# Second and third unit of a fast convolution: PSUM copies ahead of SiLU calls on ScalarE, and three matmuls of the next unit in front of product 6

## The chip, the cores and the metric

The kernel runs on one core of one Trainium2 chip. The metric is device time in microseconds (us) for one execution. A core has five engines with a queue each: TensorE (PE in the profile; its weight loads are listed apart as PEld), VectorE (DVE), ScalarE (ACT), GpSimd (POOL) and SyncE (SP), which here only issues DMAs. An engine runs its instructions in the order in which they stand in the program; between engines, semaphores say when an instruction may start.

## The reference

A convolution over the sequence with three taps, a batch normalisation with given mean and variance, and SiLU:

```python
B, S, C = 2, 2048, 1024; K = 3
xp = jnp.pad(x, ((0, 0), (1, 1), (0, 0)))
y = sum(jnp.einsum('bsc,cd->bsd', xp[:, k:k + S, :], w[k]) for k in range(K))
y = (y - mean) * (g / jnp.sqrt(var + 1e-5)) + b
return silu(y)
```

x is 2 x 2048 x 1024, w is 3 x 1024 x 1024, all in bfloat16.

## The kernel before

**The method.** Six output rows at a time are made from eight input rows by a Winograd scheme F(6,3). One sequence gives 342 such tiles of six rows. The input is transformed into eight planes (T_sb, one per batch entry); the three taps of the weights are turned into eight planes too, of which planes 0 and 7 are raw taps (wch) and planes 1 to 6 are sums and differences that GpSimd makes (uch). For each plane a product over the 1024 input channels follows, and the eight products are combined into six output rows.

**Units.** A unit is 128 output channels (dc, 0 to 7) of one batch entry (bi, 0 or 1). Units run in the order (0,0), (0,1), (1,0), (1,1), ...; here they are counted from 0, so "the second and third unit" are units 1 and 2. Units 0 to 14 are made by `unit`; the last one has code of its own (`last_part`). Each of a unit's eight products is eight accumulating matmuls of 128 x 342 (`mms`, L255), which `mms` yields one by one, so that `run(gen, n)` can emit n matmuls of a unit between other work.

**One unit.** It has four PSUM banks, A, B_, C_ and G; even and odd units use different halves of the eight. The products come in the order 1, 3, 2, 4, 5, 7, 6, 0. Product 1 goes to A and ScalarE copies it out (m1), then product 2 is added onto it in A, so product 2 must wait for copy m1. In the same way product 4 follows copy m3 (bank B_) and product 6 follows copy m5 (bank C_). Copies s1 and s2 save A after product 2 and B_ after product 4. VectorE combines all this into the six rows y (L296), in a tile `y` that has one buffer for all units, and at last ScalarE applies SiLU with the normalisation's scale and shift (L266) into yT.

**The queue of ScalarE.** The three SiLU calls of a unit (rows 2 and 4; rows 1, 3 and 5; row 0) are not issued at the unit's end but put on the list `late`. The next unit takes them from there: ahead of each of its five copies, in the order m1, m3, s1, s2, m5, `copy_out` takes as many entries of `late` as the tuple `pace` says, and after m5 the rest is taken (`while late`). `late` also holds, behind the SiLU calls, the issue of the unit's output (a transposing DMA and stores, L425 to L443, all on SyncE's queue) and, in unit 1, the scaled tap w0x (L151, ScalarE) with GpSimd's last sums for the next weights.

**Unit 0 and the transforms.** Unit 0 is emitted in pieces between the transforms. While the second batch entry is transformed (17 windows, three transforms each, 51 in all, counted by gi), `want` says how many matmuls of unit 0 are out after each transform. Unit 0 also splits products 7 and 0 by columns: a first part comes early, and eight narrow matmuls of 128 x 111 of product 7 stand just before product 6. Behind the transforms, L409 to L411 issue weight loads on SyncE, and L412 emits the rest of unit 0. Units 1 to 14 follow in a loop (L454 to L484); ahead of a unit with bi = 0 stands VectorE's sum of two taps (L169), ahead of one with bi = 1 the scaling of taps on ScalarE (L151) and GpSimd's sums.

Of the kernel before, what the change touches and what calls it, by code (L numbers as in the profile page):

```python
# [37 lines left out]
def kernel(  # L38
# [14 lines left out]
    CT = C // P  # L53
# [30 lines left out]
    def load_weights(dp):  # L84
        open_weights(dp)
        for k in (0, 2, 1):
            nc.sync.dma_start(out=pair_tile[dp][:, k], in_=w_all[:, k, :, dp * 2 * P:(dp + 1) * 2 * P])
# [160 lines left out]
    def mms(bk, j, dc, bi, c0, c1, start, at=0):  # L248

        for ct in range(CT):  # L250
            if j in (0, 7):
                lhsT = raw[dc][0 if j == 0 else 2][:, ct, :]
            else:
                lhsT = wts[dc][:, j - 1, ct, :]
            nc.tensor.matmul(  # L255
                ps_all[:, bk * 512 + at:bk * 512 + at + c1 - c0],
                lhsT=lhsT,
                rhs=T_sb[bi][:, ct, j, c0:c1],
                start=start and ct == 0,
                stop=ct == CT - 1,  # L260
                skip_group_check=not start,
            )
            yield
# [7 lines left out]
            scale=sk[:, dc:dc + 1],  # L271
        )

    def unit(dc, bi, c0, c1, banks, yT, late, pace=(1, 0, 1, 1, 0), cut=None, calls=None):

        nn = c1 - c0
        A, B_, C_, G = [ps_all[:, k * 512:k * 512 + nn] for k in banks]
        bA, bB, bC, bG = banks
        pace = list(pace)

        def et(name):
            return epool.tile([P, NTB], FP32, name=name)[:, 0:nn]

        m1, m3, m5, s1, s2, d1 = (et(n) for n in ("m1", "m3", "m5", "s1", "s2", "d1"))
        y_all = epool.tile([P, M_OUT, NTB], FP32, name="y")[:, :, 0:nn]
        y = [y_all[:, i if calls is None else ENDS.index(i)] for i in range(M_OUT)]

        def stt(o, i0, s, i1, op1=ALU.add):
            nc.vector.scalar_tensor_tensor(out=o, in0=i0, scalar=s, in1=i1, op0=ALU.mult, op1=op1)  # L296
            load["dve"] += 0.00123 * nn

        def copy_out(dst, src):
            for _ in range(pace.pop(0)):  # L300
                if late:
                    late.pop(0)()
            nc.scalar.copy(dst, src)  # L303
            load["act"] += 0.001 * nn

        if cut:


            p0 = et("s2")
            yield from mms(bG, 7, dc, bi, c0, c0 + cut, True)  # L310
            yield from mms(bC, 0, dc, bi, c0, c0 + cut, True)
            yield from mms(bC, 0, dc, bi, c0 + cut, c1, True, cut)
            copy_out(p0, C_)
        yield from mms(bA, 1, dc, bi, c0, c1, True)
        copy_out(m1, A)
        yield from mms(bB, 3, dc, bi, c0, c1, True)
        copy_out(m3, B_)
        yield from mms(bA, 2, dc, bi, c0, c1, False)
        copy_out(s1, A)
        stt(d1, m1, 2.0, A, op1=ALU.subtract)  # L320
        yield from mms(bB, 4, dc, bi, c0, c1, False)
        if cut:
            stt(y[0], B_, ALPHA, p0)
            stt(y[2], B_, ALPHA * 4.0, s1)
            nc.vector.tensor_tensor(y[0], A, y[0], op=ALU.add)
            stt(y[4], B_, ALPHA * 16.0, s1)
        else:
            copy_out(s2, B_)
            for i in (2, 4):
                stt(y[i], B_, ALPHA * 2.0 ** i, s1)  # L330
        stt(B_, m3, 2.0, B_, op1=ALU.subtract)
        yield from mms(bC, 5, dc, bi, c0, c1, True)
        copy_out(m5, C_)
        while late:
            late.pop(0)()
        for i in (1, 3, 5):
            stt(y[i], B_, ALPHA * 2.0 ** i, d1)
        if cut:
            yield from mms(bG, 7, dc, bi, c0 + cut, c1, True, cut)
        else:  # L340
            yield from mms(bG, 7, dc, bi, c0, c1, True)
        nc.vector.tensor_tensor(y[5], G, y[5], op=ALU.add)  # L342
        yield from mms(bC, 6, dc, bi, c0, c1, False)
        for i in (2, 4):
            stt(y[i], C_, BETA * 0.5 ** i, y[i])
        stt(G, m5, 2.0, C_, op1=ALU.subtract)
        if not cut:
            yield from mms(bA, 0, dc, bi, c0, c1, False)
        for i in (1, 3, 5):
            stt(y[i], G, BETA * 0.5 ** i, y[i])  # L350
        if cut:
            stt(y[0], C_, BETA, y[0])
        else:
            stt(y[0], s2, ALPHA, A)
            stt(y[0], C_, BETA, y[0])

        if calls is None:
            late.extend(lambda i=i: silu(dc, yT, y_all, c0, c1, *i, 2) for i in ((2, 5), (1, 6), (0, 1)))
        else:
            late.extend(lambda i=i: silu(dc, yT, y_all, c0, c1, *i) for i in calls)  # L360
# [10 lines left out]
    with tc.tile_pool(name="xwin", bufs=10) as xpool:  # L371
        first = unit(0, 0, 0, NTB, (0, 1, 2, 3), yTs[0], late, cut=11 * WT)
        for wi in range(NWIN):
            window = load_window(xpool, 0, wi)
            if wi in (3, 8, NWIN - 1):
                load_chunk(0, {3: 2, 8: 0, NWIN - 1: 1}[wi])
            for h in range(2):
                bk = (2 * wi + h) % 4 * 2 if wi < 10 else (0, 6, 4)[(2 * wi + h - 20) % 3]
                transform(0, wi, window, 4 * h, 4, bk, 2, 2 if h == 0 and wi in (4, 9) else 0)
            if wi == 0:  # L380
                turn_params()
            if wi == 5:
                open_chunk(0)
                scale_weights(0, (2,), on_gpsimd=True)
            if wi == 8:
                pair_sum(0, 0)
                pair_sum(0, 1)
                scale_weights(0, (0,), on_gpsimd=True)
                pair_sum(0, 2)

            run(first, {13: 2, 14: 2, 15: 4, 16: 8}.get(wi, 0))
        pair_tap(0, 0, ALU.add)
        scale_weights(0, (1,), on_gpsimd=True)
        for n, op in ((1, ALU.add), (0, ALU.subtract), (1, ALU.subtract), (2, ALU.add), (2, ALU.subtract)):
            pair_tap(0, n, op)
        make_params()
        load["act"] = load["dve"] = 0.0
        gi, done = 0, 0


        for wi in range(NWIN):
            window = load_window(xpool, 1, wi)
            for ct0, n in ((0, 3), (3, 3), (6, 2)):
                transform(1, wi, window, ct0, n, 4 + gi if gi < 4 else (4, 5, 6, 7, 2)[(gi - 4) % 5], 3)
                gi += 1
                want = 8 * gi // 3 if gi < 4 else 8 + 20 * (gi - 3) // (3 * NWIN - 3)
                run(first, want - done)
                done = want
        for k in (0, 2, 1):  # L409
            load_chunk(1, k)  # L410
        load_weights(1)  # L411
        run(first)  # L412

    opool = ctx.enter_context(tc.tile_pool(name="opool", bufs=3))
# [32 lines left out]
    def finish(dc, bi, yT):  # L447

        turned.append(turn(dc, bi, yT))
        if len(turned) > 1:  # L450
            store_unit(*turned.pop(0))

    late.append(lambda: finish(0, 0, yTs[0]))
    for ui, (dc, bi) in enumerate(units[1:-1], 1):  # L454
        yT = yTs[ui % 2]
        half = 4 * (ui % 2)
        if bi == 0 and dc + 1 < DC:
            outer_by_reduce(dc + 1)
        if bi == 1 and dc + 1 < DC:
            open_chunk(dc + 1)  # L460
            if dc:
                scale_weights(dc + 1)
                for n in range(3):
                    if n:
                        pair_sum(dc + 1, n)
                    for op in (ALU.add, ALU.subtract):
                        pair_tap(dc + 1, n, op)
            else:

                def sums(n, *taps):  # L470
                    scale_weights(1, taps)
                    pair_sum(1, n)
                    for op in (ALU.add, ALU.subtract):
                        pair_tap(1, n, op)

                sums(0, 2, 1)
                sums(1)
                late.append(lambda: sums(2, 0))
        calls = ((0, 2), (2, 6)) if ui == len(units) - 2 else None
        run(unit(dc, bi, 0, NTB, (half, half + 1, half + 2, half + 3), yT, late, (1, 0, 1, 1, 0) if ui > 1 else (0, 1, 1, 1, 0), calls=calls))  # L480
        if ui < len(units) - 2:
            late.append(lambda dc=dc, bi=bi, yT=yT: finish(dc, bi, yT))
        if bi == 1 and dc % 2 == 1 and (dc + 3) // 2 < DC // 2:
            load_weights((dc + 3) // 2)  # L484
# [151 lines left out]
```

## Time and profile before

| what | value |
|---|---|
| median of 3 runs | 191.39 us (191.19 to 192.15) |
| the profiled execution | 191.42 us |
| its span, first to last instruction | 189.7 us |
| mean granted TensorE clock | 0.992 |
| busy: TensorE, VectorE, GpSimd, ScalarE | 95%, 84%, 78%, 65% of the span |
| matmuls of a product, 128 x 342 | 944, starts 145 ns apart when nothing waits |
| VectorE, one combination of 128 x 342 | about 507 ns, starts 0.42 us apart |
| ScalarE, one copy of 128 x 342 | about 440 ns |

A row of a timeline gives start, length, engine, line of the kernel, operation, what is written from what, how many instructions are merged in the row, and in brackets how long the engine had been idle before it and what ended the idle time. The chain of waits gives start, length, and the engine and line that the end of the program hung on in that stretch. "issue" is a wait for nothing that the profile shows; in the chain it also stands for the part of an instruction that is not put down to a line.

The span has three parts. Up to about 35.6 us the input arrives and is transformed, with pieces of unit 0 in between. From there to 177.7 us the units run one after the other. The rest is the last unit's end.

### The profile page before, as it was taken

What the parts mean: (1) busy time and instruction counts of PE and PEld (TensorE: products, weight loads), DVE (VectorE), ACT (ScalarE), POOL (GpSimd) and SP (SyncE); (2) the same over time, 40 slices, a digit from 0 to 9 for tenths busy, and PEclk for the clock granted to TensorE, in tenths of its full rate; (3) what the DMA queues carried; (4) which work ended last, traced back from release to release, by engine and by line L of the source; (5) the groups of instructions that cost most, each with busy time, mean ns of one, the idle gap of its engine ahead of it and who ended that gap; (6) DMA issues with size and microseconds to landing.
All of it is one profiled execution on the core that took longest, in us unless ns stands there. A gap on an engine that the chain in (4) does not pass through costs nothing.

```text
span 189.7 us, 3974 instructions
## 1 busy us (share of the span) xinstructions
PE 179.5 (95%) x1424; PEld 126.5 (67%) x1424; DVE 159.2 (84%) x342; ACT 123.0 (65%) x205; POOL 148.8 (78%) x91
## 2 busy tenths in 40 slices
PE   7887999999999999999999999999999999999960
PEld 3656889766666666666666666666666666669960
DVE  6567699796999799969996999699969987879980
ACT  3787799658387827862876387648755874534680
POOL 6529999999769997999699969996999699901010
PEclk9999999999999999999999999999999999999996
DMA  5999999950609197979292889793747465656345
GB/s 131 326 351 309 334 385 262 247 132 0 124 19 202 34 209 209 208 175 208 58 200 46 191 229 205 167 204 75 164 80 157 91 147 98 137 110 154 87 114 111
DMA packets 86757, 31.72 MB, mean 167 GB/s; under 512 B 73357, under 2 KB 82578, under 8 KB 86738
## 3 DMA queue, kind: packets, MB, share of 16 engines
q1 hardware_dynamic: 86637, 31.46, 70.6%
q8 instruction: 11, 0.18, 0.4%
q14 instruction: 9, 0.07, 0.1%
q10 hardware_dynamic: 68, 0.01, 0.0%
q0 software_dynamic: 32, 0.01, 0.0%
HBM read 14.82 MB, written 8.39 MB: 122 GB/s over the span
## 4 chain that ended last, share of the span: by engine, by line
PE 74%; DVE 10%; DMA 5%; ACT 4%; issue 3%; SPq 2%; DVEq 0%; ACTq 0%
PE ps_all L255 66%; PE ps_all L230 7%; DVE y L296 6%; DMA xw<-in_x_dram 5%; SPq L215 1%; ACT T_sb L244 1%; DVE ps_all L296 1%; ACT yT L266 1%; PE ps_all L499 1%; DVE y L342 1%; DVE T_sb L246 0%; ACT s L303 0%; SPq L90 0%; ACT o_end L594 0%; DVE e L169 0%
## 5 line engine op out<-in xcount | busy, mean ns | idle before, releaser
L255 PE MATMUL ps_all<-T_sb,uch 128*128 128x342 bf16 (+2 forms) x816 | 120.8, 299 | 0.7 <-ACT m L303 0.3
L255 PEld LDWEIGHTS <-uch 128*128 128x128 bf16 x816 | 77.0, 97 | 35.3 <-issue 1.5
L266 ACT ACTIVATE yT<-y,beta,sk 128x684 bf16<-128x684 f32 (+4 forms) x46 | 44.0, 959 | 27.0 <-DVE y L296 27.0
L255 PE MATMUL ps_all<-T_sb,wch 128*128 128x342 bf16 (+4 forms) x288 | 43.7, 292 | 0.0
L296 DVE SCALAR_TENSOR_TENSOR y<-ps_all,y 128x342 f32<-128x342 f32 x90 | 41.8, 507 | 1.0
L173 POOL TENSOR_TENSOR uch<-e,wch 128x1024 bf16<-128x1024 f32 x16 | 33.9, 2134 | 9.1 <-PE ps_all L255 4.7
L173 POOL TENSOR_TENSOR uch<-e,w1x 128x1024 bf16<-128x1024 f32 x16 | 33.8, 2130 | 0.6
L173 POOL TENSOR_TENSOR uch<-eh,w1x 128x1024 bf16<-128x1024 f32 x16 | 33.8, 2132 | 0.5
L255 PEld LDWEIGHTS <-wch 128*128 128x128 bf16 x288 | 26.7, 97 | 10.9
L303 ACT COPY m<-ps_all 128x342 f32<-128x342 f32 x45 | 19.8, 442 | 19.5 <-PE ps_all L255 19.0
L244 ACT CAST T_sb<-ps_all 128x672 bf16<-128x672 f32 (+5 forms) x48 | 26.0, 619 | 5.5 <-PE ps_all L230 5.1
L230 PE MATMUL ps_all<-Rm,xw 128*128 128x168 bf16 (+1 forms) x272 | 26.4, 236 | 2.1 <-DMA xw<-in_x_dram 0.9
L246 DVE CAST T_sb<-ps_all 128x504 bf16<-128x504 f32 (+4 forms) x37 | 24.0, 694 | 5.1 <-PE ps_all L230 4.2
L230 PEld LDWEIGHTS <-xw 128*128 128x128 bf16 (+1 forms) x272 | 20.7, 99 | 7.3 <-issue 2.5
L296 DVE SCALAR_TENSOR_TENSOR y<-ps_all,d 128x342 f32<-128x342 f32 x45 | 20.3, 508 | 0.5
L163 POOL TENSOR_TENSOR eh<-w0x,wch 128x1024 f32<-128x1024 bf16 x8 | 17.0, 2128 | 1.1 <-ACT w0x L151 1.0
L296 DVE SCALAR_TENSOR_TENSOR y<-ps_all,s 128x342 f32<-128x342 f32 x31 | 14.5, 508 | 3.4 <-ACT s L303 3.2
L163 POOL TENSOR_TENSOR e<-wch,w2x 128x1024 f32<-128x1024 bf16 x8 | 17.0, 2129 | 0.0
L296 DVE SCALAR_TENSOR_TENSOR d<-m,ps_all 128x342 f32<-128x342 f32 x15 | 7.6, 508 | 10.2 <-ACT s L303 10.2
L296 DVE SCALAR_TENSOR_TENSOR ps_all<-m,ps_all 128x342 f32<-128x342 f32 x30 | 15.3, 508 | 0.0
L169 DVE TENSOR_REDUCE e<-wch 128x1024 f32<-128x2048 bf16 x6 | 13.7, 2277 | 0.0
L303 ACT COPY s<-ps_all 128x342 f32<-128x342 f32 x30 | 13.1, 435 | 0.5 <-PE ps_all L255 0.5
(69 smaller groups left out, 85.9 us busy)
## 6 DMA issues: line engine op xcount, KB each, us to landing
xw<-in_x_dram SPq DMA_DIRECT2D x30, 256.0 KB
out_dram<-o_sb SPq DMA_DIRECT2D x30, 192.0 KB
wch<-in_w_dram SPq DMA_DIRECT2D x9, 512.0 KB
out_dram<-o_sb SPq DMA_DIRECT2D x15, 120.0 KB
wch<-in_w_dram SPq DMA_DIRECT2D x6, 256.0 KB
xw<-in_x_dram SPq DMA_DIRECT2D x2, 224.0 KB
out_dram<-o_sb SPq DMA_DIRECT2D x15, 7.5 KB
out_dram<-o_sb SPq DMA_DIRECT2D x15, 0.5 KB
```

Of the source, the lines that this page charges most:

```text
L163: engine.tensor_tensor(e, a, c, op=ALU.add)
L169: nc.vector.tensor_reduce(e, taps.rearrange("p k ct d -> p ct d k"), axis=mybir.AxisListType.X, op=ALU.add)
L173: nc.gpsimd.tensor_tensor(wts[dc][:, 2 * n + (op == ALU.subtract)], outer[dc, n], odd, op=op)
L215: nc.sync.dma_start(out=xw[0:kk, :], in_=x[bi, t_lo:t_hi + 1, :])
L230: nc.tensor.matmul(banks[:, at:at + NJ * ntile], lhsT=xw[0:kk, (ct0 + c) * P:(ct0 + c + 1) * P], rhs=Rm[0:kk, :, 0:ntile], start=True, sto ...
L244: nc.scalar.copy(dst, src)
L246: nc.vector.tensor_copy(dst, src)
L255: nc.tensor.matmul(ps_all[:, bk * 512 + at:bk * 512 + at + c1 - c0], lhsT=lhsT, rhs=T_sb[bi][:, ct, j, c0:c1], start=start and ct == 0, st ...
L266: nc.scalar.activation(yT[:, i0:i1:step, c0:c1], y_all[:, i0:i1:step], ACT.Silu, bias=beta[:, dc:dc + 1], scale=sk[:, dc:dc + 1],)
L296: nc.vector.scalar_tensor_tensor(out=o, in0=i0, scalar=s, in1=i1, op0=ALU.mult, op1=op1)
L303: nc.scalar.copy(dst, src)
L342: nc.vector.tensor_tensor(y[5], G, y[5], op=ALU.add)
```

## The change

Three edits. First, in the last window of the transforms, `want` is raised by two (the last three of 51 transforms), so two more matmuls of unit 0's product 2 stand among them. Second, unit 0 is emitted up to the end of product 7, then three matmuls of product 1 of unit 1 (bank 4, unit 1's A), then product 6 of unit 0; unit 1 goes on with the other five. Third, units 1 and 2 have other paces:

| unit | pace before | ScalarE's order before | pace after | ScalarE's order after |
|---|---|---|---|---|
| 1 | 0,1,1,1,0 | m1, SiLU, m3, SiLU, s1, SiLU, s2, m5 | 0,0,0,1,1 | m1, m3, s1, SiLU, s2, SiLU, m5, SiLU |
| 2 | 1,0,1,1,0 | SiLU, m1, m3, SiLU, s1, SiLU, s2, m5 | 0,1,1,1,0 | m1, SiLU, m3, SiLU, s1, SiLU, s2, m5 |

Units 3 to 14 keep 1,0,1,1,0. The order on VectorE, GpSimd and SyncE is the same in both.

```diff
-    def unit(dc, bi, c0, c1, banks, yT, late, pace=(1, 0, 1, 1, 0), cut=None, calls=None):
+    def unit(dc, bi, c0, c1, banks, yT, late, pace=(1, 0, 1, 1, 0), cut=None, calls=None, begun=None):
...
-        yield from mms(bA, 1, dc, bi, c0, c1, True)
+        yield from begun or mms(bA, 1, dc, bi, c0, c1, True)
...
-                want = 8 * gi // 3 if gi < 4 else 8 + 20 * (gi - 3) // (3 * NWIN - 3)
+                want = 8 * gi // 3 if gi < 4 else 8 + 20 * (gi - 3) // (3 * NWIN - 3) + 2 * (gi > 3 * NWIN - 3)
...
         load_weights(1)
+
+        run(first, 7 * CT - done)
+        begun = mms(4, 1, *units[1], 0, NTB, True)
+        run(begun, 3)
         run(first)
...
+    paces = {1: (0, 0, 0, 1, 1), 2: (0, 1, 1, 1, 0)}
...
-        run(unit(..., yT, late, (1, 0, 1, 1, 0) if ui > 1 else (0, 1, 1, 1, 0), calls=calls))
+        run(unit(..., yT, late, paces.get(ui, (1, 0, 1, 1, 0)), None, calls, begun if ui == 1 else None))
```

More of the change, by code (lines that the diff above doesn't have):

```diff
@@ L479 @@
         calls = ((0, 2), (2, 6)) if ui == len(units) - 2 else None
-        run(unit(dc, bi, 0, NTB, (half, half + 1, half + 2, half + 3), yT, late, (1, 0, 1, 1, 0) if ui > 1 else (0, 1, 1, 1, 0), calls=calls))
+        run(unit(dc, bi, 0, NTB, (half, half + 1, half + 2, half + 3), yT, late, paces.get(ui, (1, 0, 1, 1, 0)), None, calls, begun if ui == 1 else None))
         if ui < len(units) - 2:
```

## The prediction

> **What bounds the kernel now.** Times are microseconds on the clock of the profiled execution. I write pk for product k, "copy m1" for the ScalarE copy that makes m1, and SiLU-a, -b, -c for the three SiLU calls of a unit (rows 2 and 4; 1, 3 and 5; 0). Units count from 0, so the change's second and third unit are units 1 and 2.
>
> The page first: TensorE is busy almost throughout, so a gain must come out of its waits.
>
> ```profile
> PE 179.5 (95%) x1424; PEld 126.5 (67%) x1424; DVE 159.2 (84%) x342; ACT 123.0 (65%) x205; POOL 148.8 (78%) x91
> ```
>
> Where those waits are, the timeline of weight loads (PEld) shows, since a load runs one matmul ahead and stops with it. Between the last transform and the end of the last unit but one it has four idle marks that matter:
>
> ```profile
> 39.30 4.59 PEld L255 LDWEIGHTS <-uch 128*128 128x128 bf16 x32 [0.25 <-issue]
> 44.08 0.96 PEld L255 LDWEIGHTS <-uch 128*128 128x128 bf16 x7 [0.18 <-issue]
> 52.65 1.40 PEld L255 LDWEIGHTS <-uch 128*128 128x128 bf16 x10 [0.49 <-issue]
> 62.15 1.84 PEld L255 LDWEIGHTS <-uch 128*128 128x128 bf16 x13 [0.27 <-issue]
> ```
>
> In matmul starts (145 ns apart when nothing waits) these are 0.30 before p6 of unit 0, 0.13 before p4 of unit 1, 0.44 before p2 of unit 2, 0.22 before p2 of unit 3: 1.09 together. From 62.15 to 177.7 there is no further wait. So the time is set by when p2 of unit 3 starts; all behind it follows at a fixed distance.
>
> What sets 62.15, the chain of waits in order of time answers. Up to about 37.6 it runs on TensorE; then it leaves it:
>
> ```profile
> 43.16 1.37 DVE y L296 x3
> 44.57 1.13 issue
> 45.70 0.42 ACT s L303
> 46.12 0.49 ACT yT L266
> 46.61 0.42 ACT s L303
> 47.06 0.94 DVE y L296 x2
> ...
> 53.60 0.37 issue
> 53.96 0.79 DVE e L169
> 54.76 1.40 issue
> 56.16 0.50 DVE d L296
> ...
> 60.28 0.51 DVE y L296
> 60.81 0.17 ACT yT L266
> 60.98 0.70 issue
> 61.68 0.43 ACT m L303
> 62.15 115.58 PE ps_all L255 x816
> ```
>
> This is the heart of it. From 47.06, the first write of y in unit 1, VectorE works without a break through unit 1, the tap sum (L169) and unit 2 until y4 of unit 2 is final at 60.78; then SiLU-a of unit 2 and copy m1 of unit 3 behind it on ScalarE, then TensorE. The waits at 39, 44 and 52 are not on this chain: had TensorE not lost them, it would have stood longer before 62.15. And 47.06 is set by ScalarE:
>
> ```profile
> 42.73 0.96 ACT L266 ACTIVATE yT<-y,beta,sk 128x684 bf16<-128x684 f32 x1 [0.47 <-DVE y L296]
> 43.60 0.42 ACT L303 COPY m<-ps_all 128x342 f32<-128x342 f32 x1
> 44.55 1.24 ACT L266 ACTIVATE yT<-y,beta,sk 128x1026 bf16<-128x1026 f32 x1 [0.53 <-DVE y L296]
> 45.70 0.42 ACT L303 COPY s<-ps_all 128x342 f32<-128x342 f32 x1
> 46.02 0.67 ACT L266 ACTIVATE yT<-y,beta,sk 128x342 bf16<-128x342 f32 x1
> 46.59 0.43 ACT L303 COPY s<-ps_all 128x342 f32<-128x342 f32 x1
> ```
>
> SiLU-a, m3, SiLU-b, s1, SiLU-c, s2, and y at 47.06, 0.04 after s2 ends. The tile y has one buffer, so unit 1 may not write it before SiLU-c of unit 0 has read it.
>
> **The change, part by part.**
>
> *Two matmuls of p2 into the last window's transforms.* The matmul at 35.06 is followed by a transform only at 35.31 (0.25 instead of 0.145), because a ScalarE eviction ends at 35.28. Two more there put that transform at 35.06 + 3 x 0.145 = 35.50, and the five transforms left still take 0.24. The wait of 0.11 is covered: everything after is 0.11 earlier. The last evictions end at 36.13 instead of 35.95, and p1 of unit 1 reads them only from 38.9.
>
> *Three matmuls of p1 (unit 1) before p6 (unit 0).* The last narrow matmul of p7 starts at 38.95 and lets go at 39.00; p6 starts at 39.30, behind copy m5 (38.81 + 0.44 = 39.25). Three times 0.145 = 0.44 covers the wait of 0.30. The bank that they write was evicted by 36. With the 0.11, p6 starts at 38.89 + 0.44 = 39.33, and p1 has three done: its last start is 41.07 instead of 41.48, 0.41 earlier. VectorE's work on p6 is not delayed, as it reaches it only at 41.8.
>
> *SiLU calls of unit 1 moved back.* The new ScalarE order is m1, m3, s1, SiLU-a, s2, SiLU-b, m5, SiLU-c, w0x. A copy starts 0.035 after its last matmul's modelled end (0.307 behind that start). m1: 41.07 + 0.34 = 41.41. m3: p3 ends 1.16 later, 42.57; it is done at 43.0, so p4 no longer waits (0.13 gone). s1 needs p2: 43.74. From there ScalarE is back to back, with start-to-start times read from the rows: copy 0.33, SiLU-a 0.87, SiLU-b 1.15. SiLU-a 43.74 + 0.33 = 44.07; s2 44.94 (p4 ready at 44.90); SiLU-b 45.27 (its rows are final at 44.4); m5 46.42 (p5 ready at 46.06); SiLU-c 46.75, plus its 0.67 is 47.42. The first y follows 0.04 later: **47.44 to 47.46 instead of 47.06, 0.39 later**. What is lost: ScalarE idles from 43.0 to 43.7 with SiLU-a's data ready at 42.6, and m5 now stands ahead of SiLU-c. In the order as built, the y write waits for exactly that SiLU-c.
>
> Behind the moved calls: TensorE's p6 of unit 1 needs m5 (ends 46.85) and comes at 47.04, so no wait. The transposing DMA of unit 0 on the sync queue starts 0.7 later (46.76 before); ScalarE reuses its source only near 61. w0x starts at 47.32 instead of 47.25, and GpSimd's taps (48.40 before) follow by 0.07: the last two end at 52.8 and 54.9, wanted by p5 and p6 of unit 2 at about 54.2 and 56.5. Cost nothing; without that cover, 0.07.
>
> *SiLU-a behind copy m1 in unit 2.* TensorE reaches unit 2 at 49.36 (49.88 before), m1 runs at 50.72, p2 starts at 51.69 without its 0.44. VectorE is 0.39 later, so SiLU-a runs at 51.30 + 0.39 = 51.69, m3 behind it at 52.56 to 53.0, and p4, due at 52.85, waits 0.2. SiLU-b and -c follow VectorE (53.5, 54.97), s1 and s2 end at 55.1 and 56.0; VectorE asks for them only at 56.55 and 56.97, since it is in the tap sum. Nothing of this reaches the chain.
>
> *Unit 3.* VectorE's unbroken stretch is shifted whole: y4 final at 61.17, SiLU-a, copy m1 at 62.07, p2 at **62.15 + 0.39 = 62.54**. TensorE was ready at about 61.2 and stands 1.3.
>
> Sum: waits removed 0.11 + 0.30 + 0.13 + 0.44 + 0.22, all given back in one wait before p2 of unit 3, and 0.39 more. The span goes from 189.7 to 190.1. The profiled execution took 191.42 with that span, the runs' median is 191.39; so 191.4 + 0.4 = **191.8**.
>
> Two prices are not in the trace. A y write released by a SiLU call instead of a copy: the neighbour is 0.04 after s2, the ends are 0 and 0.4 (a whole copy time); I take 0.04. A copy followed at once by the two-row SiLU: the neighbours (before the one-row call) give 0.32 and 0.33; ends 0.2 and 0.45. Both shift the sum by -0.2 to +0.5 at most.
>
> **Rivals.**
>
> *The waits simply go (190.2).* If VectorE were not bound, the five waits, 1.2, come off: 191.4 - 1.2. For it: each is plainly a copy behind a SiLU call or a matmul behind a copy, and the change reorders just these. It needs y of unit 1 to start by about 46, thus SiLU-c not to be waited for. Against: the chain above has VectorE unbroken from 47.06 to 60.8.
>
> *TensorE's head start does not come (192.2).* If p6 still waits and the tail gains nothing, s1 is ready 0.41 later, and as ScalarE's run starts with s1, y comes 0.39 + 0.41 later: 191.4 + 0.8. Against: the copy m5 and the evictions are long done by the trace.
>
> *The clock drops in the new wait (193.8).* The place is the 1.3 before p2 of unit 3. In the trace TensorE's last matmul ends at 185.2 and the granted clock is 0.83 from 186 to 187 and 0.50 after, so some 1.5 after work stopped; if 1.3 is enough, it decides. At the start the matmuls ran at half rate (140 ns instead of 72) from 1.2 to about 5.2, so 4 at half rate lose 2: 191.8 + 2. Against: the wait of 1.34 between matmuls at 182.94 left the clock at 1.00. The Trainium skill (TensorE: Matmul & The Clock Gate, Part 1, the HAM clock gate) says that the clock falls only after an idle window of about 3.4 us, free-running; by that this gap keeps full clock and the sum stays 191.8, though the trace's own drop came sooner than 3.4 behind the last matmul.
>
> **How the numbers follow.** Forecast 0.80, alone 191.3 to 192.3 (the two unknown prices, and the scatter of 191.19 to 192.15 before); waits go 0.07; no head start 0.08; clock 0.05. The range 191.1 to 192.4 holds the forecast and most of the third. Half a per cent, 0.96, is about what a measurement of this kernel tells from no change: under 190.4 lies the first rival and a trace of the forecast, 0.08; above 192.35 the clock, half of the missing head start, and 0.03 of the forecast, 0.12; the rest, 0.80, within.
>
> **What would show it.** Right: no TensorE wait near 39, 44 and 52; the first y of unit 1 after SiLU-c, near 47.4; VectorE unbroken to 61; one wait of about 1.3 before p2 of unit 3, with TensorE unbroken from 62.5. Wrong: y of unit 1 before 47.0, or that wait under 0.9; a clock under 1.0 after 62.

## The result and the profile after

The changed kernel takes 192.12 us (median of 9 runs, 191.62 to 192.56) beside 191.40 us of the kernel before (9 runs, 191.19 to 192.42). The ratio is 1.0035, 95% interval 1.0019 to 1.0051: slower by 0.7 us, with an interval of 0.4 to 1.0. The profiled execution took 192.52 us, with a span of 190.7 (before 189.7).

Terms are those of the prediction: pk is product k, SiLU-a, -b, -c are a unit's three SiLU calls. In the profiles of the kernels with the change, line numbers have moved down by one or two (the copies, L303 before, are L304 or L305; the combinations, L296 before, are L297 or L298; the matmuls, L255, can be L256).

First the page. TensorE does the same 1424 matmuls, over a longer span:

```profile
PE 178.6 (94%) x1424; PEld 126.0 (66%) x1424; DVE 159.2 (83%) x342; ACT 123.0 (64%) x205; POOL 148.8 (78%) x91
```

The timeline of the weight loads of the changed kernel, 50 to 66 us, with the idle time in brackets:

```profile
53.71 2.13 PEld L255 LDWEIGHTS <-uch 128*128 128x128 bf16 x15 [0.31 <-issue]
...
63.22 2.85 PEld L255 LDWEIGHTS <-uch 128*128 128x128 bf16 x20 [1.43 <-issue]
```

The four waits of before (near 39, 44, 52 and 62) have become two: 0.26 before p4 of unit 2, and 1.39 before p2 of unit 3 (in matmul starts beyond 145 ns). From 63.22 to the last unit TensorE runs without a break, as it did from 62.15 before.

Why p2 of unit 3 is late, ScalarE and VectorE tell. ScalarE in the changed kernel, from copy m1 of unit 1 on:

```profile
42.03 0.45 ACT L304 COPY m<-ps_all 128x342 f32<-128x342 f32 x1 [0.37 <-PE ps_all L255]
43.24 0.45 ACT L304 COPY m<-ps_all 128x342 f32<-128x342 f32 x1 [0.76 <-DVE y L297]
44.41 0.45 ACT L304 COPY s<-ps_all 128x342 f32<-128x342 f32 x1 [0.73 <-PE ps_all L255]
44.75 0.96 ACT L266 ACTIVATE yT<-y,beta,sk 128x684 bf16<-128x684 f32 x1
45.61 0.43 ACT L304 COPY s<-ps_all 128x342 f32<-128x342 f32 x1
45.93 1.25 ACT L266 ACTIVATE yT<-y,beta,sk 128x1026 bf16<-128x1026 f32 x1
47.08 0.44 ACT L304 COPY m<-ps_all 128x342 f32<-128x342 f32 x1
47.40 0.68 ACT L266 ACTIVATE yT<-y,beta,sk 128x342 bf16<-128x342 f32 x1
```

and VectorE's first write of y in unit 1:

```profile
48.12 0.94 DVE L297 SCALAR_TENSOR_TENSOR y<-ps_all,s 128x342 f32<-128x342 f32 x2 [2.26 <-ACT yT L266]
```

ScalarE stands idle 0.73 ahead of s1 with SiLU-a's rows final, then works back to back; SiLU-c ends at 48.08, y starts 0.03 later, and VectorE has stood 2.26 for it. From 48.12 VectorE runs unbroken to y4 of unit 2, and the last link is again ScalarE, where copy m1 of unit 3 stands behind SiLU-a of unit 2:

```profile
61.88 0.96 ACT L266 ACTIVATE yT<-y,beta,sk 128x684 bf16<-128x684 f32 x1 [2.03 <-DVE y L297]
62.74 0.77 ACT L304 COPY m<-ps_all 128x342 f32<-128x342 f32 x2
```

The chain of waits of this profile must be read with care here, since between 53.70 and 62.01 it runs over TensorE and not over VectorE:

```profile
53.70 8.30 PE ps_all L255 x56
62.01 0.02 issue
62.03 0.02 ACTq L304
62.04 0.70 issue
62.74 0.43 ACT m L304
```

From m1 the chain goes back to a semaphore instruction that comes just before it in time and that was released when product 3 of unit 3 ended, at 62.01. By the program it is copy m3 that waits for product 3, not m1: product 1, which m1 copies, had ended at 60.83. The 0.70 of "issue" is the time in which m1 stands in the queue behind SiLU-a, which started at 61.88, as soon as y4 was final. So an earlier product would not have started m1 sooner; an earlier y4 would have. The chain also passes the wait of p4 of unit 2 at 53.70; that this wait is not the cause is shown by experiments 2, 4 and 6, which do not have it and in which p2 of unit 3 follows the first y all the same.

**Two sources of the 1.1 in the span.** The first matmul of the last transformed window starts at 34.88 before and at 35.38 after. The program up to that matmul is the same in both kernels; the 0.50 between them is the arrival of the input. The load on which the chain of waits hangs ends at 13.85 before and 14.35 after:

```profile
7.28 6.57 DMA xw<-in_x_dram
```

```profile
7.62 6.73 DMA xw<-in_x_dram
```

In the ten profiles of this study that matmul starts between 34.75 and 35.84, early and late with and without the change (35.44 in the kernel of experiment 5, which has no part of the change). So the two stages are read apart: below, "work" is the time from that matmul to VectorE's last copy at the end of the program (L604 before, L611 after; behind it follow the last stores, 4.3 to 4.8). Work was 150.37 before and is 150.95 after: **0.58 is the change, 0.50 is scatter of the input.**

### The profile page after: what moved, and what is told of

Read it like the earlier page. It is cut to its first block, busy times and chain, and to the rows that moved or that the text cites. A ratio compares the mean times of both kernels' runs of the same rounds, so it can differ in the third digit from the quotient of the medians.

```text
span 190.7 us, 3972 instructions
## 1 busy us (share of the span) xinstructions
PE 178.6 (94%) x1424; PEld 126.0 (66%) x1424; DVE 159.2 (83%) x342; ACT 123.0 (64%) x205; POOL 148.8 (78%) x91
## 4 chain that ended last, share of the span: by engine, by line
PE 81%; DMA 5%; ACT 5%; DVE 3%; SPq 2%; issue 2%; ACTq 0%; DVEq 0%
PE ps_all L255 73%; PE ps_all L230 7%; DMA xw<-in_x_dram 5%; ACT yT L266 2%; DVE y L297 2%; SPq L215 1%; ACT T_sb L244 1%; PE ps_all L506 1%; ACT m L304 1%; SPq L90 1%; DVE T_sb L246 0%; ACT o_end L601 0%; ACT s L304 0%; DVE y L343 0%; DVE ps_all L297 0%
## 5 line engine op out<-in xcount | busy, mean ns | idle before, releaser
L255 PE MATMUL ps_all<-T_sb,uch 128*128 128x342 bf16 (+2 forms) x816 | 120.7, 299 | 1.5 <-ACT m L304 1.2
L255 PEld LDWEIGHTS <-uch 128*128 128x128 bf16 x816 | 76.9, 97 | 35.9 <-issue 2.0
L255 PE MATMUL ps_all<-T_sb,wch 128*128 128x342 bf16 (+4 forms) x288 | 43.7, 292 | 0.0
L297 DVE SCALAR_TENSOR_TENSOR y<-ps_all,y 128x342 f32<-128x342 f32 x90 | 41.8, 507 | 1.0
L255 PEld LDWEIGHTS <-wch 128*128 128x128 bf16 x288 | 26.7, 97 | 10.9
L304 ACT COPY m<-ps_all 128x342 f32<-128x342 f32 x45 | 19.8, 443 | 21.4 <-PE ps_all L255 20.2
L230 PE MATMUL ps_all<-Rm,xw 128*128 128x168 bf16 (+1 forms) x272 | 25.8, 233 | 2.9 <-DMA xw<-in_x_dram 1.8
L297 DVE SCALAR_TENSOR_TENSOR y<-ps_all,d 128x342 f32<-128x342 f32 x45 | 20.3, 508 | 0.5
L297 DVE SCALAR_TENSOR_TENSOR y<-ps_all,s 128x342 f32<-128x342 f32 x31 | 14.5, 508 | 5.2 <-ACT s L304 2.8
L297 DVE SCALAR_TENSOR_TENSOR ps_all<-m,ps_all 128x342 f32<-128x342 f32 x30 | 15.3, 508 | 0.0
L297 DVE SCALAR_TENSOR_TENSOR d<-m,ps_all 128x342 f32<-128x342 f32 x15 | 7.6, 506 | 8.7 <-ACT s L304 8.7
L304 ACT COPY s<-ps_all 128x342 f32<-128x342 f32 x30 | 13.1, 437 | 1.0 <-PE ps_all L255 1.0
```

The costliest lines, as they stand in the source:

```text
L230: nc.tensor.matmul(banks[:, at:at + NJ * ntile], lhsT=xw[0:kk, (ct0 + c) * P:(ct0 + c + 1) * P], rhs=Rm[0:kk, :, 0:ntile], start=True, sto ...
L255: nc.tensor.matmul(ps_all[:, bk * 512 + at:bk * 512 + at + c1 - c0], lhsT=lhsT, rhs=T_sb[bi][:, ct, j, c0:c1], start=start and ct == 0, st ...
```

## The experiments

All were timed in five rounds beside the kernel before. Ratios are to that kernel on the same chip; "first y" and "work" are from one profiled execution of each kernel, counted from the first matmul of the last window.

| kernel | median us (before) | ratio, 95% interval | first y | work |
|---|---|---|---|---|
| before | | | 12.18 | 150.37 |
| changed | 192.12 (191.40) | 1.0035 (1.0019 to 1.0051) | 12.74 | 150.95 |
| 1 changed, y of unit 1 in its own tile | 190.63 (191.35) | 0.9964 (0.9945 to 0.9983) | 10.69 | 149.28 |
| 2 changed, old order in unit 1 | 191.32 (191.35) | 1.0001 (0.9985 to 1.0017) | 12.18 | 150.46 |
| 3 new orders alone | 192.82 (191.35) | 1.0073 (1.0044 to 1.0102) | 13.03 | 151.24 |
| 4 changed, SiLU-a before s1, SiLU-c before m5 | 191.22 (191.35) | 0.9989 (0.9967 to 1.0012) | 11.85 | 150.06 |
| 5 before, y of unit 1 in its own tile | 191.59 (191.59) | 0.9998 (0.9978 to 1.0018) | 12.17 | 150.37 |
| 6 changed, SiLU-c before m5 | 191.87 (191.59) | 1.0013 (0.9996 to 1.0030) | 12.40 | 150.60 |
| 7 new orders, y in its own tile, nothing put ahead | 190.59 (191.59) | 0.9957 (0.9937 to 0.9976) | 10.99 | 149.59 |
| 8 as 1, without the two matmuls among the transforms | 190.17 (191.59) | 0.9930 (0.9905 to 0.9954) | 10.69 | 149.29 |

Work repeats well: 5 agrees with before, and 8 with 1, within 0.01. Set beside the timed ratios, the change of work lies within the interval in every row but that of 1, where it is some 0.04 us beyond.

The theory: the first y of unit 1 sets the time, because VectorE works from there without a break up to what p2 of unit 3 waits for. The rivals: TensorE's removed waits count one by one, and the loss lies elsewhere; or the loss is in the input stage.

**1. Unit 1's y in a tile of its own.** It lies where the input windows were, and lives until unit 2 is emitted; the buffers of the program's end are placed later for it. Nothing else changes.

```diff
-        y_all = epool.tile([P, M_OUT, NTB], FP32, name="y")[:, :, 0:nn]
+        y_all = ybuf.get((dc, bi), epool).tile([P, M_OUT, NTB], FP32, name="y")[:, :, 0:nn]
...
+    ystack = ExitStack()
+    ybuf[units[1]] = ystack.enter_context(tc.tile_pool(name="ypool", bufs=1))
     for ui, (dc, bi) in enumerate(units[1:-1], 1):
...
+        if ui == 2:
+            ystack.close()
```

> The changed kernel, with unit 1's y in a tile of its own, so that it need not wait for unit 0's SiLU-c. Theory (the first y of unit 1 sets the time through VectorE's unbroken stretch): y starts after copy s2, near 45.4 on the clock of the kernel before instead of 47.06; all waits of TensorE go, p2 of unit 3 starts near 61.0, and the time is 1.0 to 1.2 below before, about 190.3. Rival 1 (the loss is in the wait of p4 behind copy m3 in unit 2, or in ScalarE's new order as such): the order is unchanged, so the time stays 0.4 to 0.7 above before. Rival 2 (the loss is in the input stage, which ended 0.5 later in the changed kernel's profiled execution): the same 0.4 to 0.7 above before, with the last transform late again.

The first y moves from 12.74 to 10.69 and waits for copy s2 now; VectorE's row says so:

```profile
46.53 0.94 DVE L298 SCALAR_TENSOR_TENSOR y<-ps_all,s 128x342 f32<-128x342 f32 x2 [0.22 <-ACT s L305]
```

and the chain of waits of this kernel has one piece from the last transform to the last unit but one:

```profile
36.86 140.74 PE ps_all L256 x995
```

No wait of TensorE is left. Work falls by 1.67 against the changed kernel and by 1.09 against before, which is the sum of before's four waits. The timed median fell by 0.7 (interval 0.33 to 1.05), where 1.0 to 1.2 was expected: that the kernel is faster is clear from the times, the full 1.09 rests on the trace. ScalarE's order and the input stage are as in the changed kernel (its input was the latest of all, 35.84), so neither rival can hold.

**2. The old order in unit 1, the rest of the change kept.**

```diff
-    paces = {1: (0, 0, 0, 1, 1), 2: (0, 1, 1, 1, 0)}
+    paces = {1: (0, 1, 1, 1, 0), 2: (0, 1, 1, 1, 0)}
```

> The changed kernel with ScalarE's old order in unit 1 only; the matmuls put ahead and unit 2's new order stay. Theory: the first y of unit 1 is again set by SiLU-b, s1, SiLU-c, s2 behind unit 0's last y rows, and comes at 46.96 to 47.06; the matmuls ahead buy nothing, as TensorE waits for VectorE before p2 of unit 3 anyway: before -0.1 to 0.0, 191.3 to 191.4. Rival 1 (each wait of TensorE removed counts): 0.30 and 0.44 stay removed, 0.7 below before. Rival 2 (input stage): 0.4 to 0.7 above before.

First y 12.18, as before to the hundredth; ratio 1.0001. TensorE no longer waits 0.30 before p6 of unit 0 nor 0.44 before p2 of unit 2, and nothing is won: it waits 0.42 before p4 of unit 1 instead of 0.13, and 0.66 before p2 of unit 3 instead of 0.22. The rows of the two waits:

```profile
44.45 2.13 PEld L255 LDWEIGHTS <-uch 128*128 128x128 bf16 x15 [0.47 <-issue]
62.54 1.54 PEld L255 LDWEIGHTS <-uch 128*128 128x128 bf16 x11 [0.71 <-issue]
```

This is the plainest case of a gain off the path. It also shows that the loss up to p2 of unit 3 is unit 1's new order, all of it: counted from the first matmul of the last window, p2 of unit 3 starts 27.27 after it before, 27.28 here and 27.84 in the changed kernel. Work is 0.09 above before all the same; nearly all of that arises behind p2 of unit 3, and it is not explained.

**3. The new orders, no matmul put ahead.**

```diff
-        run(unit(..., (1, 0, 1, 1, 0) if ui > 1 else (0, 1, 1, 1, 0), calls=calls))
+        run(unit(..., {1: (0, 0, 0, 1, 1), 2: (0, 1, 1, 1, 0)}.get(ui, (1, 0, 1, 1, 0)), calls=calls))
```

> The kernel before with ScalarE's new orders in units 1 and 2 only; no matmul is put ahead. Theory: ScalarE's run starts with copy s1, which waits for p2 of unit 1, and this is 0.4 later without the head start; the first y comes at 47.7 to 47.9, 0.6 to 0.8 above before, that is slower than the changed kernel by up to 0.4. Rival 1 (each wait of TensorE removed counts): 0.13, 0.44 and 0.22 go, 0.8 below before. Rival 2 (input stage made late by the matmuls moved into it): no difference from before.

First y 13.03, work 0.87 above before, ratio 1.0073: the slowest of all. (The median is 1.5 above; 0.87 lies at the lower end of the interval, 0.8 to 2.0.) In the new order ScalarE's run starts with s1, which TensorE releases, so there the head start does count: 0.29 between this kernel and the changed one.

**4. SiLU-a before s1, and SiLU-c before m5.**

```diff
-    paces = {1: (0, 0, 0, 1, 1), 2: (0, 1, 1, 1, 0)}
+    paces = {1: (0, 0, 1, 1, 1), 2: (0, 1, 1, 1, 0)}
```

> The changed kernel with unit 1's order m1, m3, SiLU-a, s1, SiLU-b, s2, SiLU-c, m5: SiLU-a fills the time in which ScalarE stood idle, and SiLU-c goes ahead of m5. Theory: SiLU-a at 42.9, s1 at 43.8, SiLU-b at 44.4 when its rows are final, s2, SiLU-c to 46.6; the first y at 46.6 to 46.7, 0.4 below before, 191.0. Rival 1 (each wait of TensorE removed counts, and the copies must be ahead of the SiLU calls): like the changed kernel. Rival 2 (input stage): 0.4 to 0.7 above before.

Rows of ScalarE in unit 1:

```profile
42.95 0.96 ACT L266 ACTIVATE yT<-y,beta,sk 128x684 bf16<-128x684 f32 x1
43.81 0.43 ACT L304 COPY s<-ps_all 128x342 f32<-128x342 f32 x1
44.43 1.24 ACT L266 ACTIVATE yT<-y,beta,sk 128x1026 bf16<-128x1026 f32 x1 [0.19 <-DVE y L297]
```

The idle time ahead of s1 is filled, SiLU-b waits only for its own rows, and the first y comes at 11.85, 0.33 before the kernel before. Work is 0.31 lower, where 0.4 was expected. The timing, 0.9989, has 1 within its interval; it cannot tell 0.3 from nothing, so the gain stands on the trace alone.

**5. The kernel before with y in a tile of its own** (the edit of 1 on the kernel before).

> The kernel before, with unit 1's y in a tile of its own and nothing else changed. Theory: in the old order copy s2 stands behind all three SiLU calls, and the first y waits for s2 too, so it still comes 12.2 after the first transform of the last window: no difference from before, 191.4. Rival (the single buffer by itself is what holds VectorE, whatever ScalarE's order): y comes 0.4 earlier or more, and the time falls by as much.

First y 12.17, work 150.37: no difference. In the old order s2 stands behind all three SiLU calls, and y, which starts 0.03 after s2 here too, gains nothing from a free tile. (The first y reads s1 and the bank, not s2; that it waits for s2 is what the traces of before, 1 and 5 show, and why is not shown.) The buffer binds only once s2 stands ahead of a SiLU call.

**6. SiLU-c before m5.**

```diff
-    paces = {1: (0, 0, 0, 1, 1), 2: (0, 1, 1, 1, 0)}
+    paces = {1: (0, 0, 0, 1, 2), 2: (0, 1, 1, 1, 0)}
```

> The changed kernel with SiLU-c of unit 0 ahead of copy m5 in unit 1 instead of behind it. Theory: the first y comes one copy (0.33) earlier than in the changed kernel, 0.23 later than before, and the time is 0.2 above before, 191.6; TensorE waits about 0.4 before p6 of unit 1, which costs nothing. Rival (TensorE's waits count): that new wait of 0.4 comes on top of the changed kernel's time.

First y 0.34 earlier than in the changed kernel, work 0.35 lower: one copy's place in the queue, passed on in full. TensorE waits 0.48 before p6 of unit 1 for the later m5, at no cost. The first y of experiment 4 is another 0.55 earlier, so SiLU-a ahead of s1, in the time in which ScalarE stood idle, is worth more than the place of m5.

**7. The new orders and the free tile, no matmul put ahead** (the edits of 3 and 1 on the kernel before).

> The kernel before with the new orders in units 1 and 2 and unit 1's y in a tile of its own; no matmul put ahead. Theory: VectorE no longer binds, so TensorE's waits count one by one: all go but the 0.30 before p6 of unit 0, so 0.7 to 0.8 below before, 190.6, and 0.3 above the kernel that has the matmuls put ahead too. Rival (the matmuls put ahead never matter): the same time as with them, 1.1 below before.

Work 0.78 below before, 0.3 above kernel 1: the only wait that TensorE has left behind the transforms is the one before p6 of unit 0, 0.30. With VectorE off the path this wait of TensorE costs its length.

**8. Kernel 1 without the two matmuls moved among the transforms.**

```diff
-                want = ... + 2 * (gi > 3 * NWIN - 3)
+                want = ...
```

> The changed kernel with unit 1's y in a tile of its own, and without the two matmuls moved into the last window's transforms; the three matmuls ahead of p6 stay. Forecast's step (they cover a wait of 0.11 for an eviction): 0.1 above the kernel that has them. Rival (the pause of about 0.1 comes with the change to the narrow last window's weights, whatever stands before it): no difference, within 0.03 from the first transform of the last window to the end, and 1.1 below before.

Work 149.29 against 149.28: those two matmuls buy nothing. The timed ratios of 1 and 8, each to the kernel before beside it, differ by 0.34%, some 0.65 us, which the traces do not show behind the input stage. The two intervals overlap only just, so whether 8 is faster than 1 stays open. Kernels 1, 7 and 8 are faster than the kernel before, by 0.4 to 0.7%.

## Why the prediction was right, and by how much it was off

- **The bound.** VectorE's unbroken stretch sets p2 of unit 3: right. In kernels 2 to 6, from 0.85 later to 0.32 earlier, the start of p2 of unit 3 follows the first y within 0.02, and work follows it within 0.1, whatever TensorE's waits did.
- **Unit 1's order.** The run of ScalarE was forecast as 3.71 from s1 to y (43.74 to 47.45) and took 3.71 (44.41 to 48.12). The two prices that the trace before did not show were right as well: copy to SiLU-a 0.34, SiLU-c to y 0.03.
- **The size.** First y was forecast 0.39 later and came 0.56 later, since s1 itself came 0.17 later than worked out. The step that failed is the first term, "the wait of 0.11 is covered": I had put the pause ahead of the narrow transforms down to an eviction on ScalarE that ended 0.03 before. In the changed kernel the same eviction ends at 35.78, 0.32 before that transform, and the pause is still there, behind three matmuls as behind one; experiment 8 gives the gain as 0.01. That is 0.10. Another 0.05 is the handover: m3 and s1 start 0.08 to 0.09 after their last matmul's modelled end (m3: 43.15 to 43.24), not 0.035 as m1 does (42.00 to 42.03). The trace has a semaphore instruction of its own ahead of m3 and of s1, which ends 0.04 before the copy starts, and none ahead of m1; that this is the reason is likely, but no run tests it. (The row of m3 puts the end of its wait down to VectorE; in experiment 3 the same row names TensorE, with the same 0.08.) The last 0.02 is not accounted for.
- **The three matmuls put ahead.** p6 of unit 0 no longer waits, as forecast. The head start is worth 0.3 (7 against 1, and 3 against the changed kernel), not 0.41, which had the false 0.11 in it.
- **Unit 2.** m1 ahead of SiLU-a took the 0.44 away, and p4 waited 0.26 (0.2 forecast) behind m3; neither reached the end.
- **The given-back wait.** 1.39 before p2 of unit 3 (1.3 forecast).
- **The rivals.** "The waits simply go" needed y not to wait for SiLU-c: experiment 1 makes that true, and its work falls by the four waits, 1.09. "The head start does not come" is experiment 3: 0.87 over before, 0.8 forecast. The clock did not fall: the row below is the changed kernel's stretch of the new wait (its third number from the right is the granted clock).

```profile
61.80:63.20 1.40, 0.19 (x2) 0.00 (x0) 1.36 (x5) 1.32 (x3) 1.40 (x1) 1.00 0.86 192
```

The Trainium skill (TensorE: Matmul & The Clock Gate, Part 1, the HAM clock gate) lets the clock fall only after an idle window of about 3.4 us; a wait of 1.39 at clock 1.00 agrees with that without testing it, and the fall some 1.5 us after the last matmul, which the prediction names, came sooner than that window.

- **The time.** 191.8 was forecast, 192.12 measured. Of the 0.32 between them, the late first y accounts for 0.17. The work accounts for 0.58 of the 0.72 between the medians; the interval of 0.4 to 1.0 includes it.

## What to carry to other kernels

A wait of the busiest engine is worth its length only if nothing else arrives later at the next place where engines meet: before removing one, follow the chain on the engine that releases it, as an unbroken stretch there takes every earlier gain back. When calls are moved back in a queue, look for who waits for the last of them, above all for a tile with one buffer, and for idle time left where they stood. Where both the order and the buffer hold a start, an edit of one alone can show nothing or a loss: here the free tile alone changed nothing (5), the new orders alone lost 0.87 (3), and both together gained 0.78 (7). Try them together.

## What the runs showed of the hardware

The weight loads of the last window have 33 rows instead of 128, and the first of them does not run ahead of the matmuls as the others do. It starts only 0.004 us before its own matmul, whether one matmul (kernel before, first rows) or three (changed kernel, second rows) stand before it. The idle marks of 0.16 and 0.28 differ because in the changed kernel the last 128-row load itself ran one matmul ahead:

```profile
35.06 0.10 PEld L255 LDWEIGHTS <-uch 128*128 128x128 bf16 x1
35.31 0.19 PEld L230 LDWEIGHTS <-xw 33*128 33x128 bf16 x5 [0.16 <-issue]
```

```profile
35.56 0.26 PEld L255 LDWEIGHTS <-uch 128*128 128x128 bf16 x3
36.10 0.20 PEld L230 LDWEIGHTS <-xw 33*128 33x128 bf16 x5 [0.28 <-issue]
```

The matmul before it is followed after 0.252 and 0.238 us instead of 0.145, and leaving the narrow loads costs about 0.09 again (0.118 and 0.120 between matmuls of 48 columns and the next, where 0.025 is usual between themselves). Two more passages into 33-row loads in the kernel before lose as much: the matmul at 20.73 is followed after 0.194 instead of 0.099, the one at 34.71 after 0.168 instead of 0.072. So each passage between 128-row and 33-row loads that was looked at costs some 0.1 us here. Why the load is held is not shown.
